# Block sums' rows for groups 4 to 7 copied by GpSimd, the last output piece cut in two, planner constants 35.0/6.2 to 33.0/6.0

## The chip, the cores and the metric

One core of one Trainium2 chip runs the kernel. The metric is the device time of one execution in microseconds (us); the time given for a kernel is the median of its runs. The engines are TensorE (PE, matrix products; its weight loads are listed apart as PEld), VectorE (DVE), ScalarE (ACT), GpSimd (POOL) and SyncE (SP), which here issues nearly all DMA transfers. Every engine works through its own list of instructions in the order in which the program wrote them; between engines there are semaphores.

## What is computed

Local attention with block sums for 4 batches of 8 heads, 768 positions and width 64, and behind it a feed-forward net on the 3072 token rows. Each query sees the keys less than 16 positions away and 24 "sum" keys, one for each block of 32 positions: the maximum of the block's keys, with the mean of the block's values.

```python
k_sum = k.reshape(B, H, nb, block, D).max(axis=3)
v_sum = v.reshape(B, H, nb, block, D).mean(axis=3)
scores = concatenate([where(mask_l, scale * q @ k.T, -1e9), scale * q @ k_sum.T + log(block)])
a = softmax(scores);  attn = a @ concatenate([v, v_sum])
h = x @ w_in;  r = maximum(h, 0);  out = (r * r) @ w_out      # x: attn as 3072 x 512, w_in: 512 x 2048
```

## The kernel before, in words

**Tiling.** The 3072 tokens are 48 groups of 64 (`TQ`), 12 groups to a batch. Eight groups make a unit of 512 tokens, of which there are six (`NU`). The attention of a unit writes its result as two float32r parts, `xh` and `xl`, and the feed-forward net then runs over 16 column blocks `f` of the hidden layer: `FI` (line 799, 12 products of 128x128 by 128x512) makes a block of the hidden layer, ACT and DVE square and split it, and `FO` (line 828, 12 products) adds it to the output `o`, which stays in PSUM for the whole unit: two tiles of 128 x 4 x 256, each with two of the unit's four output tiles of 128 rows.

**Attention of one group g** (below 8): `QL` loads the queries, `S` (line 483) makes scores in PSUM, `X` (line 554, DVE) their maximum, `E` (line 570, ACT) four exponentials with their sums, `R` (lines 582 and 583, DVE) the inverse sums, `N` (line 589, POOL) multiplies by them, `T` (line 601, PE) transposes, `A` (line 608, ACT) copies the transpose out of PSUM, `V` (line 645, PE) multiplies with the values, and `XH` and `XL` (lines 697 and 700, DVE) write `xh` and `xl`. `KC` (line 493, POOL) moves the 24 sum keys beside the next group's window, so `S` of the next group waits for it. The right side of `V` needs the group's own 94 value rows, loaded by `LV` (line 446), and the 24 rows of block means in the same tile `vv`. Those means are made once per batch: `FV` loads the values, `VM` (line 412, PE) averages them, `VS` (line 424, ACT) copies them to the tile `vs`. From there `LS` brings them into each `vv`: for groups 0 to 3 as a copy on POOL (line 452), for groups 4 to 7 and for later groups that need it as a DMA that SP issues (line 449).

**Weights.** They come as 64-bit floats. In unit 0 each block is loaded (`WL`, line 742, 512 KB each), taken apart and put together by ACT and DVE (`WM` 745, `WR` 748, `WJ` 754, `WH` 759, `WW` 762) before its `FI` or `FO`. Groups 8 to 15 are attended to in the same stretch.

**Order.** `Plan.order` simulates the five engines with a cost for each task and writes the instructions out in the order in which its tasks start. Among the tasks that are ready on a free engine it takes the one with the lowest key, which is a due time. The due times of the first eight groups are fixed (`wanted`: -20 + 2j for group j); those of the feed-forward items, of the weights and of all later groups hang on `T0`, `SLOW` and `STEP` (line 266). A load ends, in this simulation, when all bytes queued before it have moved at 300,000 bytes per us, and 1.9 us later. A task is ready 0.12 us (`HOP`) after the last of those it comes after. At one instant the engines are served in the order in which the tasks first named them: POOL, SP, DVE, PE, ACT. Keys near the change: `LS` of a group g below 8 has 2g - 39, `KC` 2g - 35, `N` 2g - 30, `T` 2g - 29, `V` 2g - 20; `S` of group 8 is above 29.

**The end.** `FO` of the last block runs in two pieces of six products, one for each tile of `o`. Behind each piece `put` copies the first output tile with DVE and the second with ACT (line 863) and stores both (line 872); the very last tile is copied half by DVE and half by ACT.

Of the kernel before, what the change touches and what calls it, by code (L numbers as in the profile page):

```python
# [10 lines left out]
F32 = mybir.dt.float32  # L11
# [9 lines left out]
P = 128  # L21
# [7 lines left out]
UG = 8  # L29
# [68 lines left out]
class Plan:  # L98
# [13 lines left out]
    def add(self, name, engine, cost, emit, key, after=(), take=(), use=(), size=0, begin=0.0, behind=None):  # L112
        t = Task(name, engine, cost, emit, key, [a for a in after if a is not None], list(take), list(use), size, begin)
        t.behind = behind
        t.index = len(self.tasks)
        self.tasks.append(t)
        for b in t.take + t.use:
            b.users.append(t)
        return t
# [67 lines left out]
def attention_then_relu2_ffn(  # L187
# [75 lines left out]


    items = [(u, f) for u in range(NU) for f in range(NF)]
    T0, SLOW, STEP, LEAD = 35.0, 6.6, 6.2, 1.5
    unit_at = [T0 + NF * (SLOW * min(u, 1) + STEP * max(u - 1, 0)) for u in range(NU + 1)]
    at_item = {(u, f): unit_at[u] + f * (STEP if u else SLOW) for u, f in items}

# [161 lines left out]
    def loads(g):  # L431

        b, w = divmod(g, NW)
        k0 = first_key(w, S)
        due = wanted(g)
        q, vv = q_bufs[g], v_bufs[g]
        early = g < EARLY
        lq = t_QL[g] = add(
            f"QL{g}", "SP", 0.45, lambda: nc.sync.dma_start(out=q.tile, in_=qW[g]), due - (26 if early else 50), take=[q],
            size=2 * P * DM, begin=due - (45 if early else 65),  # L440
        )

        def load_v():

            for r0, r1 in ((0, 96),) if k0 + 96 <= S else ((0, 64), (64, LOC)):
                nc.sync.dma_start(out=vv.tile[NB + r0 : NB + r1, :], in_=vS[b, k0 + r0 : k0 + r1, :])

        def load_s():
            nc.sync.dma_start(out=vv.tile[:NB, :], in_=vs_bufs[b].tile)

        def copy_s():
            nc.gpsimd.tensor_copy(out=vv.tile[:NB, :], in_=vs_bufs[b].tile)

        lv = t_LV[g] = [
            add(f"LV{g}", "SP", 0.45, load_v, due - 20, behind=lq if early else None, take=[] if early else [vv],
                use=[vv] if early else [], size=4 * LOC * DM, begin=due - 36)
        ]
        if g < EARLY or w < NV or (b == 0 and g < EARLY + NV):
            ts = t_VS[b]
            if g >= UG // 2:  # L460
                lv.append(add(f"LS{g}", "SP", 0.45, load_s, due - 19, ts + lv, use=[vv, vs_bufs[b]], size=4 * NB * DM))
            else:
                lv.append(add(f"LS{g}", "POOL", 0.45, copy_s, due - 19, ts + lv, use=[vv, vs_bufs[b]]))
# [320 lines left out]
    def ffn(u, f, o, done):  # L784
# [38 lines left out]
        def o_of(o, t):  # L823
            return o[t // 2].tile.rearrange("p (a b) c -> p a (b c)", a=2)[:, t % 2]
# [9 lines left out]
        todo = [(t, i) for t in range(NTT) for i in range(3)]  # L834
        if first or last:
            pieces = [[x for x in todo if x[0] // 2 == t] for t in range(NTT // 2)]
        else:
            pieces = [sorted(todo, key=lambda x: x[1] == 2)]
        for i, piece in enumerate(pieces):
            t6 = add(  # L840
                f"FO{u}_{f}_{i}", "PE", 0.2325 * len(piece), lambda piece=piece: outer(piece), due + 0.1 * i,
                [t4, t5] + t_W[1, f] + done[-1:] + [x for g in range(UG, FIRST_S) for x in t_M[g]] * (u == f == 0),
                take=[o[i]] if first else [], use=[gh, gl] + ([] if first else [o[i]] if last else o),
            )
            done.append(t6)
            if last:
                put(u, i, o[i], lambda t: o_of(o, t), t6, due + 0.1 * i)

    def put(u, i, o, o_of, t, due):

        x = buf("t", 3, (P, 2 * DM), F32, f"os{u}_{i}")
        rows = u * TU + 2 * i * P
        t2 = None
        for k in range(2):

            end = u == NU - 1 and i == NTT // 2 - 1 and k
            copies = (("DVE", 0, DM),), (("ACT", 0, DM),), (("DVE", 0, DM // 2), ("ACT", DM // 2, DM))
            ts = []
            for e, a, b in copies[2 if end else k]:

                def copy(e=e, a=a, b=b, k=k):
                    f = nc.scalar.copy if e == "ACT" else nc.vector.tensor_copy
                    f(out=x.tile[:, k * DM + a : k * DM + b], in_=o_of(2 * i + k)[:, a:b])  # L863

                t2 = add(
                    f"PC{u}_{2 * i + k}{e}", e, 0.1 + 0.0012 * (b - a), copy, due + 0.6, [t], take=[] if t2 else [x],
                    use=[o] + [x] * bool(t2), behind=t2,
                )
                ts.append(t2)

            def store(k=k):
                nc.sync.dma_start(
                    out=out[rows + k * P : rows + (k + 1) * P, :], in_=x.tile[:, k * DM : (k + 1) * DM]
                )

            add(f"PS{u}_{2 * i + k}", "SP", 0.45, store, due + 1, ts, use=[x], size=4 * P * DM)


    batch_k(0)
# [84 lines left out]
```

## Time and profile before

| what | us |
|---|---|
| median of three runs (lowest, highest) | 637.24 (636.46, 638.43) |
| the profiled execution, whole | 638.7 |
| its span, first to last instruction | 637.0 |
| PE busy in the span | 615.8 |
| DVE, ACT, POOL busy | 296.7, 267.9, 75.1 |

The page of the profile gives for each engine its busy time, and for groups of instructions the line, the operation and the tiles (`out<-in`). A row of a timeline has the start, the duration, the engine, the line, the operation, its tiles, shapes and count; in brackets stands how long the engine sat idle before it and what ended that. The chain of waits is the sequence of work that ended last, followed back from the end: a row has its start, its duration and the engine with its line. "issue" there is time in which the engine waited for nothing that the profile shows. Lent buffers appear as `qvpa_lent`. The clock is that granted to TensorE, as a share of full speed (2.4 GHz). A row of a table of stretches has the stretch and its length, then for PE, PEld, DVE, ACT and POOL the busy us and the instructions, the clock, the busy share of the DMA engines and what they moved.

### The profile page before, as it was taken

The numbers are of one execution on the slowest core, as the hardware profiler recorded it, in microseconds if no ns is written. First come the engines' busy times: TensorE is split into PE (matmuls) and PEld (weight loads), VectorE is DVE, ScalarE is ACT, GpSimd is POOL, SyncE is SP. The second block draws the span as 40 slices with busy tenths as digits, with TensorE's granted clock in tenths as the row PEclk, the third lists the DMA queues.
The fourth block names the chain that finished last, engine by engine and source line by source line (L and its number), as shares of the span: only waits on it lengthen the run. The fifth ranks groups of instructions, "written<-read, shape, count | busy, mean of one in ns | idle before, by whom it ended". The sixth has DMA issues, their size and how long they took to land.

```text
span 637.0 us, 10957 instructions
## 1 busy us (share of the span) xinstructions
PE 615.8 (97%) x4192; PEld 491.2 (77%) x4192; DVE 296.7 (47%) x513; ACT 267.9 (42%) x701; POOL 75.1 (12%) x136
## 2 busy tenths in 40 slices
PE   5779999999999999999999999999999999999997
PEld 3568777778787778778778787788788778888885
DVE  3789789725422543534543554435354442322221
ACT  2778678736544453423432523424243332222221
POOL 4520002011101110101201001101011010000000
PEclk9989999999999999999999999999999999999999
DMA  8978896435233834133222742333233120100001
GB/s 286 278 246 274 288 342 196 144 78 157 75 83 78 267 85 122 56 78 89 71 80 66 241 135 73 83 87 88 88 87 84 29 66 1 67 0 1 0 2 66
DMA packets 55592, 73.84 MB, mean 116 GB/s; under 512 B 6524, under 2 KB 33148, under 8 KB 55540
## 3 DMA queue, kind: packets, MB, share of 16 engines
q1 hardware_dynamic: 55540, 73.15, 39.0%
q8 instruction: 33, 0.54, 0.4%
q14 instruction: 19, 0.16, 0.1%
HBM read 55.56 MB, written 16.78 MB: 114 GB/s over the span
## 4 chain that ended last, share of the span: by engine, by line
PE 93%; DVE 2%; DMA 2%; issue 1%; POOL 1%; SPq 0%; ACT 0%; DVEq 0%; ACTq 0%; POOLq 0%
PE h L799 42%; PE o L828 42%; PE att L483 3%; PE x L645 3%; DMA kb<-kT 2%; PE s L483 1%; PE vps L412 1%; PE att L645 0%; DVE kb L358 0%; PE t L601 0%; DVE nm L554 0%; SPq L355 0%; POOL qvpa_lent L589 0%; POOL kb L493 0%; DVE xh L697 0%
## 5 line engine op out<-in xcount | busy, mean ns | idle before, releaser
L799 PE MATMUL h<-xh,w 128*128 128x512 f32 x768 | 243.6, 398 | 3.0 <-DVE nm L582 1.9
L828 PE MATMUL o<-w,gh 128*128 128x512 f32 x768 | 200.6, 396 | 0.6 <-ACT os L863 0.6
L799 PEld LDWEIGHTS h<-xh,w 128*128 128x128 f32 x768 | 144.4, 189 | 38.1 <-issue 2.8
L828 PEld LDWEIGHTS o<-w,gh 128*128 128x128 f32 x768 | 142.9, 188 | 36.1 <-issue 2.7
L799 PE MATMUL h<-xl,w 128*128 128x512 f32 x384 | 152.6, 397 | 0.0
L807 ACT ACTIVATE r<-h 128x512 f32<-128x512 f32 x96 | 57.4, 598 | 206.6 <-PE h L799 206.4
L818 DVE TENSOR_TENSOR gl<-r,gh 128x512 fp32r<-128x512 f32 x96 | 67.1, 699 | 100.0 <-ACT gh L815 62.5
L813 DVE TENSOR_TENSOR r<-r 128x512 f32<-128x512 f32 x64 | 45.2, 706 | 139.0 <-ACT r L807 138.9
L828 PE MATMUL o<-w,gl 128*128 128x512 f32 x384 | 109.1, 391 | 0.0
L799 PEld LDWEIGHTS h<-xl,w 128*128 128x128 f32 x384 | 72.6, 189 | 17.5 <-DVE xl L700 0.2
L828 PEld LDWEIGHTS o<-w,gl 128*128 128x128 f32 x384 | 72.2, 188 | 15.9
L815 ACT CAST gh<-r 128x512 fp32r<-128x512 f32 x96 | 59.5, 620 | 53.7 <-DVE r L813 26.2
L570 ACT ACTIVATE p<-p,nm 128x118 f32<-128x118 f32 x160 | 60.9, 383 | 30.1 <-DVE nm L554 30.0
L589 POOL TENSOR_TENSOR p<-p,nm 128x472 f32<-128x472 f32 x40 | 42.8, 1070 | 116.8 <-DVE nm L583 83.6
L493 POOL COPY kb<-kb 128x96 f32<-128x96 f32 x44 | 16.0, 364 | 311.1 <-PE att L483 302.8
L538 DVE SCALAR_TENSOR_TENSOR p<-att,mask 128x472 f32<-128x472 f32 x38 | 23.4, 645 | 28.7 <-PE att L483 28.7
L618 DVE STREAM_TRANSPOSE a<-p 128x512 f32<-128x512 f32 x40 | 28.3, 707 | 10.4 <-POOL p L589 7.8
L570 ACT ACTIVATION_READ_ACCUMULATOR p<-p,nm 128x1 f32 x160 | 30.0, 188 | 0.0
L554 DVE TENSOR_REDUCE nm<-p 128x4 f32<-128x472 f32 x40 | 25.1, 636 | 0.2
L483 PE MATMUL att<-kb,q 64*64 64x118 f32 x608 | 24.1, 274 | 0.2 <-POOL kb L493 0.2
L697 ACT CAST xh<-x 128x512 fp32r<-128x512 f32 x20 | 11.7, 583 | 29.9 <-PE x L645 29.9
L762 DVE TENSOR_TENSOR w<-t,w 128x1024 fp32r<-128x1024 f32 (+1 forms) x18 | 21.3, 1187 | 4.3 <-ACT w L759 4.3
(56 smaller groups left out, 332.9 us busy)
## 6 DMA issues: line engine op xcount, KB each, us to landing
raw<-wW SPq DMA_DIRECT2D x32, 512.0 KB
turn<-a SPq DMA_DIRECT2D x160, 64.0 KB
a<-turn SPq DMA_DIRECT2D x40, 256.0 KB
v<-vS SPq DMA_DIRECT2D x36, 192.0 KB
kb<-kT SPq DMA_DIRECT2D x16, 384.0 KB
out<-os SPq DMA_DIRECT2D x24, 256.0 KB
q<-qW SPq DMA_DIRECT2D x40, 128.0 KB
fv<-vS SPq DMA_DIRECT2D x18, 256.0 KB
```

Of the source, the lines that this page charges most:

```text
L483: nc.tensor.matmul(score_tile(g)[c * TQ : (c + 1) * TQ, j, :], lhsT=q_bufs[g].tile[rows, p, :] if term else unscale[rows, :], rhs=kb[rows, ...
L538: nc.vector.scalar_tensor_tensor(out=pr.tile[:, js, :KEYS], in0=score_tile(g)[:, js], scalar=SCALE, in1=mask_of(g)[0].unsqueeze(1).broadca ...
L554: nc.vector.tensor_reduce(out=m, in_=score_tile(g)[:, js] if by_pe else pr.tile[:, js, :KEYS], op=ALU.max, axis=AX.X, negate=True)
L570: nc.scalar.activation(x, score_tile(g)[:, p] if by_pe else x, AF.Exp, bias=nm.tile[:, p : p + 1], scale=SCALE if by_pe else 1.0, accum_ou ...
L589: nc.gpsimd.tensor_tensor(out=x, in0=x, in1=nm.tile[:, 2 * NPAIR :].unsqueeze(2).broadcast_to([P, NPAIR, KEYS]), op=ALU.mult)
L618: nc.vector.transpose(out=a.tile.rearrange("p (j n r) -> p j n r", j=NSQ, n=NPAIR), in_=pr.tile.rearrange("p n (j c) -> p j n c", c=SQ),)
L799: nc.tensor.matmul(h.tile, lhsT=lhs.tile[:, k * P : (k + 1) * P], rhs=rhs[:, k, c0 : c0 + TU], start=(i == 0), stop=(i == 3 * KT - 1),)
L807: t2 = add(f"RL{u}_{f}", "ACT", 0.62, lambda: nc.scalar.activation(r.tile, h.tile, AF.Relu), due + 3, [t1], take=[r], use=[h])
L813: lambda: nc.vector.tensor_tensor(out=r.tile, in0=r.tile, in1=r.tile, op=ALU.mult), due + 4, [t2], use=[r],
L815: t4 = add(f"GH{u}_{f}", "ACT", 0.62, lambda: nc.scalar.copy(out=gh.tile, in_=r.tile), due + 5, [t3], take=[gh], use=[r])
L818: lambda: nc.vector.tensor_tensor(out=gl.tile, in0=r.tile, in1=gh.tile.bitcast(F32), op=ALU.subtract),
L828: nc.tensor.matmul(o_of(o, t), lhsT=terms[i][0].tile[:, t * P : (t + 1) * P], rhs=terms[i][1].tile, start=(first and i == 0), stop=(last a ...
```

## The change

Three things. `T0` goes from 35.0 to 33.0 and `STEP` from 6.2 to 6.0, so all due times that hang on them move. `LS` of groups 4 to 7 becomes a POOL copy like that of groups 0 to 3. In the last unit the second piece of the last `FO` is cut into two of three products, one for each output tile; `put` now works on one output tile, which one engine copies whole (DVE the even, ACT the odd ones), also at the very end.

```diff
-    T0, SLOW, STEP, LEAD = 35.0, 6.6, 6.2, 1.5
+    T0, SLOW, STEP, LEAD = 33.0, 6.6, 6.0, 1.5
...
-            if g >= UG // 2:
+            if not early:
                 lv.append(add(f"LS{g}", "SP", 0.45, load_s, due - 19, ts + lv, use=[vv, vs_bufs[b]], size=4 * NB * DM))
             else:
                 lv.append(add(f"LS{g}", "POOL", 0.45, copy_s, due - 19, ts + lv, use=[vv, vs_bufs[b]]))
...
             pieces = [[x for x in todo if x[0] // 2 == t] for t in range(NTT // 2)]
+            if last and u == NU - 1:
+                pieces[-1:] = pieces[-1][:3], pieces[-1][3:]
...
         for i, piece in enumerate(pieces):
+            tiles = [t for t in range(NTT) if any(x[0] == t for x in piece)]
+            k = tiles[0] // 2
             t6 = add(
                 f"FO{u}_{f}_{i}", "PE", 0.2325 * len(piece), lambda piece=piece: outer(piece), due + 0.1 * i,
                 [t4, t5] + t_W[1, f] + done[-1:] + [x for g in range(UG, FIRST_S) for x in t_M[g]] * (u == f == 0),
-                take=[o[i]] if first else [], use=[gh, gl] + ([] if first else [o[i]] if last else o),
+                take=[o[k]] if first else [], use=[gh, gl] + ([] if first else [o[k]] if last else o),
             )
             done.append(t6)
-            if last:
-                put(u, i, o[i], lambda t: o_of(o, t), t6, due + 0.1 * i)
...
-            end = u == NU - 1 and i == NTT // 2 - 1 and k
-            copies = (("DVE", 0, DM),), (("ACT", 0, DM),), (("DVE", 0, DM // 2), ("ACT", DM // 2, DM))
...
+            for t in tiles if last else ():
+                put(u, t, o[k], lambda t=t: o_of(o, t), t6, due + 0.1 * t)
...
+        copy = nc.scalar.copy if k else nc.vector.tensor_copy
+        t1 = add(
+            f"PC{u}_{t}", "ACT" if k else "DVE", 0.62 if k else 0.7, lambda: copy(out=part(), in_=o_tile()), due + 0.6, [t6],
+            take=[] if k else [x], use=[o] + [x] * k, behind=t_PC[-1] if k else None,
+        )
+        t_PC.append(t1)
+        add(
+            f"PS{u}_{t}", "SP", 0.45, lambda: nc.sync.dma_start(out=out[rows : rows + P, :], in_=part()), due + 1, [t1],
+            use=[x], size=4 * P * DM,
+        )
```

## Rows read from the trace of the kernel before

**Rows 1.** The page, part 1: busy us of each engine.
```profile
PE 615.8 (97%) x4192; PEld 491.2 (77%) x4192; DVE 296.7 (47%) x513; ACT 267.9 (42%) x701; POOL 75.1 (12%) x136
```
**Rows 2.** Three stages; columns: stretch, length, busy by engine, clock, DMA share, GB/s.
```profile
0.00:41.70 41.70, 27.03 (x496) 20.08 (x497) 24.68 (x65) 23.86 (x92) 19.88 (x62) 0.96 0.97 286
41.70:147.50 105.80, 104.45 (x696) 82.64 (x697) 81.32 (x116) 72.46 (x152) 12.51 (x15) 0.98 0.66 213
147.50:637.00 489.50, 484.29 (x3002) 388.53 (x3000) 190.71 (x333) 171.57 (x458) 42.73 (x59) 1.00 0.29 80
```
**Rows 3.** The same view in short stretches ahead of the feed-forward's start.
```profile
26.70:29.40 2.70, 0.18 (x5) 0.04 (x1) 1.69 (x5) 1.73 (x8) 1.63 (x3) 1.00 1.04 262
29.40:33.00 3.60, 3.56 (x47) 2.85 (x47) 1.36 (x3) 1.62 (x7) 0.31 (x2) 0.53 0.99 307
39.90:43.20 3.30, 1.47 (x6) 1.14 (x7) 3.27 (x8) 1.74 (x6) 0.98 (x1) 1.00 1.04 323
43.20:46.60 3.40, 3.40 (x9) 2.69 (x9) 3.40 (x6) 2.26 (x4) 0.00 (x0) 0.50 0.30 95
```
**Rows 4.** The chain of waits up to the first feed-forward product.
```profile
26.88 2.56 issue
...
36.79 0.98 POOL qvpa_lent L589
...
39.16 0.71 PE att L645 x16
...
41.73 10.24 PE h L799 x36
```
**Rows 5.** DMA queues, 26.6 to 29.5 us: packets, MB, share of 16 engines.
```profile
q8 instruction: 1, 0.02, 2.4%
```
**Rows 6.** Timeline of POOL.
```profile
18.64 1.16 POOL L452 COPY qvpa_lent<-vs 24x512 f32<-24x512 f32 x2
...
23.11 0.97 POOL L589 TENSOR_TENSOR qvpa_lent<-qvpa_lent,nm 128x472 f32<-128x472 f32 x1 [0.59 <-DVE nm L583]
...
26.16 0.97 POOL L589 TENSOR_TENSOR qvpa_lent<-qvpa_lent,nm 128x472 f32<-128x472 f32 x1 [1.40 <-DVE nm L583]
...
28.61 0.97 POOL L589 TENSOR_TENSOR qvpa_lent<-qvpa_lent,nm 128x472 f32<-128x472 f32 x1 [1.07 <-DVE nm L583]
```
**Rows 7.** Timeline of SP: the first DMA copy of sum rows.
```profile
25.02 0.89 SPq L449 DMA_DIRECT2D qvpa_lent<-vs  x1
```
**Rows 8.** Timeline of DVE.
```profile
23.19 1.44 DVE L754 SCALAR_TENSOR_TENSOR t<-t,raw 128x512 uint32<-128x512 uint32 x1
...
35.38 0.42 DVE L697 CAST xh<-att 128x256 fp32r<-128x256 f32 x1 [0.69 <-PE att L645]
...
36.28 0.16 DVE L582 TENSOR_SCALAR nm<-nm 128x4 f32<-128x4 f32 x1
...
38.09 0.69 DVE L754 SCALAR_TENSOR_TENSOR t<-t,raw 128x512 uint32<-128x512 uint32 x1
...
39.89 0.42 DVE L697 CAST xh<-att 128x256 fp32r<-128x256 f32 x1 [0.52 <-PE att L645]
```
**Rows 9.** Timeline of PE: the longest idle time after the start.
```profile
82.81 0.50 PE L799 MATMUL h<-xh,w 128*128 128x512 f32 x1 [1.13 <-DVE w L762]
```
**Rows 10.** Timelines of PE, DVE and ACT at the end.
```profile
630.59 0.39 PE L828 MATMUL o<-w,gl 128*128 128x512 f32 x1
...
631.97 0.40 PE L828 MATMUL o<-w,gl 128*128 128x512 f32 x1
...
631.02 0.69 DVE L863 COPY os<-o 128x512 f32<-128x512 f32 x1 [6.10 <-PE o L828]
632.40 1.02 DVE L863 COPY os<-o 128x512 f32<-128x512 f32 x2 [0.69 <-PE o L828]
...
631.75 0.58 ACT L863 COPY os<-o 128x512 f32<-128x512 f32 x1 [7.87 <-DVE os L863]
633.50 0.37 ACT L863 COPY os<-o 128x256 f32<-128x256 f32 x1 [1.17 <-DVE os L863]
```

More of the change, by code (lines that the diff above doesn't have):

```diff
@@ L842, in ffn @@
                 [t4, t5] + t_W[1, f] + done[-1:] + [x for g in range(UG, FIRST_S) for x in t_M[g]] * (u == f == 0),
-                take=[o[i]] if first else [], use=[gh, gl] + ([] if first else [o[i]] if last else o),
+                take=[o[k]] if first else [], use=[gh, gl] + ([] if first else [o[k]] if last else o),
             )
             done.append(t6)
-            if last:
-                put(u, i, o[i], lambda t: o_of(o, t), t6, due + 0.1 * i)
[L849 to L854, printed above, removed]
-            end = u == NU - 1 and i == NTT // 2 - 1 and k
-            copies = (("DVE", 0, DM),), (("ACT", 0, DM),), (("DVE", 0, DM // 2), ("ACT", DM // 2, DM))
[L858 to L876, printed above, removed]
@@ new lines, in ffn, with put, part @@
+            for t in tiles if last else ():
+                put(u, t, o[k], lambda t=t: o_of(o, t), t6, due + 0.1 * t)
+    os_bufs = {}
+    def put(u, t, o, o_tile, t6, due):
+        k = t % 2
+        x = os_bufs[u, t // 2] = os_bufs.get((u, t // 2)) or buf("t", 3, (P, 2 * DM), F32, f"os{u}_{t // 2}")
+        rows = u * TU + t * P
+        def part():
+            return x.tile[:, k * DM : (k + 1) * DM]
+        copy = nc.scalar.copy if k else nc.vector.tensor_copy
[8 more added lines that the diff above has]
+        )
@@ L879, in attention_then_relu2_ffn @@
+    t_PC = []
     batch_k(0)
```

## The prediction

> **What bounds the kernel now.** I read the page's busy times first, then a table of stages, then the chain of waits and the timelines of the stretch where TensorE is not full. PE is busy 615.8 of the 637.0 us of the span, every other engine less than half [rows 1]. So only two things can move the time: when PE is idle, and when it runs slowly. The table of stages says where that is: PE is idle 41.7 - 27.0 = 14.7 us before the first feed-forward product at 41.73, 1.35 us in the rest of unit 0, and 5.2 us after 147.5, of which 4.6 lie behind the last product [rows 2, 10]. From 41.73 on the order of the work hardly matters as long as the other engines keep ahead. What the change can win is an earlier start of the feed-forward net, a better clock around it, and a shorter end.
>
> Ahead of that start three places matter. In the middle of group 3's `V`, PE stands still for 2.56 us and waits for nothing that the profile names [rows 4]; the one packet of the instruction queue q8 in that stretch starts there, in a stretch in which the DMA engines are full [rows 3, 5]. So I read it as PE waiting for its own next instructions behind data. What follows is slow: the clock is 0.53 from 29.4 to 33.0, after a stretch in which PE was busy 0.18 of 2.7 us. It happens again from 43.2 to 46.6, at 0.50, after PE was busy only 1.47 of 3.3 us; these are the first feed-forward products [rows 3]. Last, the chain that ends the attention of unit 0: `N` of group 7 on POOL at 36.79, then its `T`, `A`, its `V` at 39.16, `XH` at 39.89 or later, `FI` at 41.73 [rows 4].
>
> **The change part by part.**
>
> *Four copies from SP to POOL.* Four DMA issues go (0.89 us for the first, with a landing behind full queues [rows 7, 3]) and four POOL copies come. Two of the same shape took 1.16 us together, so one is 0.58 and four are 2.3 us [rows 6]. Their keys, 2g - 39, are below those of `N` (2g - 30), so they go in between POOL's products as soon as the planner sees `vs` and their `LV`, from about 22 us on. POOL waited there 0.59, 1.40 and 1.07 us before the products of groups 3, 4 and 5, together 3.06 us [rows 6]: room for the 2.3. Queued behind a copy on POOL are `KC` of groups 5 and 6 and `N` of groups 4 and 5; who waits for those is `S` and `T` on PE. A copy that does not fit delays these by up to 0.6 us each, but PE then stands at its missing instructions until 29.44 anyway [rows 4]. Everything up to 22 us is the same as before, the loads queued by then too, so that fetch should come back at the same time. I take 0 for the copies; without that cover they cost up to 2.3.
>
> A second price is not in that sum: DVE and POOL get in each other's way. `WJ` of 128x512 took 1.44 us while POOL worked at its side and 0.69 us alone [rows 8, 6]. Up to 0.75 for each copy is 3.0 us at most, below 0 is excluded since POOL gets no faster. I take 0 here too, as the same standstill of PE covers it, and keep 3.0 for a rival.
>
> *What that frees.* The planner let a load end only after all bytes queued before it, so it placed the `V` of groups 4 and 5 behind `S` of group 8. With the rows copied by POOL they are ready as soon as their `A` is. Their keys (-12, -10) are far below that of `S` of group 8 (above 29), so they move up, and `V` of group 6, which now stands behind `T` of group 7, goes ahead of it. The chain from `N` of group 7 stays: it depends on scores, exponentials and sums alone. What gets shorter is its end. Its inverse sums waited for DVE, which did `XH` of group 4 (35.38) and the mask of group 8 first and came to it at 36.28, at most 0.65 us late [rows 8]. At the end DVE did `XH` of group 6 at 39.89, a piece of weight work and `XL` of 6 before `XH` of 7, of which 0.42 + 0.68 + 0.34 = 1.4 us can fall away (0.68 as 0.69 of such a `WJ` [rows 8], 0.34 as an `XL` that overlaps its neighbours). `FI` cannot start before 39.16 + 0.71 + 0.42 = 40.3 without an earlier `N`. So the gain is between 0 and 41.73 - 40.3 + 0.3 = 1.7; I take 1.1, since DVE will still have some weight work in the queue.
>
> *The clock.* If `FI` starts at 40.6, PE is busy some 2.6 us of the stretch from 39.9 to 43.2 instead of 1.47. Stretches with 0.18 and 1.47 us were followed by half speed [rows 3]. At half speed 3.4 us of work lose 1.7 us; all or nothing.
>
> *Due times.* `T0` shifts the feed-forward items, weights and later groups by 2 us against the fixed first eight groups, and `STEP` stretches both sides of the later units alike. Weight tasks keep keys far above those of the first eight groups, so there is little to reorder; loads of weights can be queued some us earlier. On the path this is 0; a new order can cost or give a switch of PE here and there, which I put at 0.5 either way. After 41.7 DVE is busy 81.3 of 105.8 us [rows 2] and once PE waits 1.13 us for a `WW` [rows 9]; an earlier PE meets that sooner. I take 0.2 us given back, between 0 and 1.1.
>
> *The end.* Now the last product ends at 631.97 + 0.40 = 632.37, DVE copies tile 2 and the first half of tile 3, ACT the second half until 633.87, and 3.1 us follow until the span ends [rows 10]. In the new order both `FO` of tile 3 and the copy of tile 2 become ready 0.12 us after `FO` of tile 2, and the planner serves DVE before PE. The copy is then written first, and the question is whether the products of tile 3 wait for it. DVE waited at 631.02 for the product of 630.59, which is of the pair's second tile though the copy reads the first; `XH` of groups 4 and 6 waited likewise for the `V` of the next group in the other half of the same PSUM tile [rows 8, 10]. So waits go by the whole tile. Then: tile 2's products end at 632.37 - 0.69 = 631.68, copy to 632.41, three products from 632.45 at 0.23 apart to 633.3, ACT's 0.58 to 633.92: 0.05 later than now. If they did not wait: 632.37, ACT behind DVE (as at 631.75, right after DVE's end) from 632.44 to 633.02, a gain of 0.85. I take +0.05, and keep both ends.
>
> The Trainium skill ("PSUM — Partial Sum Buffer", "Summary: rules for kernel authors") says that PSUM may be read while products run if they target a different bank, and that one should guard by bank. The two tiles lie in different banks, so by that rule the end would be 0.85 us shorter and the forecast 634.7. The rows above speak against it here.
>
> **Sum.** Of the profiled execution's 638.7: -1.1 (start), -1.7 (clock), 0 (copies), +0.2 (given back), +0.05 (end) = 636.2. That execution lies 1.46 above the median of 637.24, almost the price of the half-speed stretch, so I suppose that the median execution has lost only part of it and count half, 0.85, against the median: 637.24 - 1.1 - 0.85 + 0.2 + 0.05 = 635.5.
>
> **The rivals.**
>
> *Nothing at the front* (637.2). DVE holds `XH` of group 7 as late as now, or PE meets weights that are not ready in its second and third block. For it: DVE is busy 3.27 of 3.3 us from 39.9 on [rows 3]. Against it: `XH` and `XL` of groups 4 and 6 really move into idle time of DVE (0.69 and 0.52 us [rows 8]). 637.24 - 0.1 = 637.2.
>
> *All of it* (633.8). `FI` at 40.0, half speed gone, and the pieces overlap: 637.24 - 1.7 - 0.85 - 0.85 = 633.8.
>
> *Copies in the way* (640.0). On POOL, between 22 and 29 us, the four copies and what they stretch on DVE (2.3 + 3.0 = 5.3 us) delay `KC`, `N` and `X` of groups 4 to 6 by more than PE's standstill of 2.56 hides; from that point on each us is an us, at most 5.3 - 2.56 = 2.7: 637.24 + 2.7 = 640.0. For it: the stretched `WJ` and a chain that passes POOL. Against it: 3.06 us of idle POOL. The Trainium skill ("GPSIMD Engine Reference", "Specifications") says that GpSimd shares its SBUF interfaces with VectorE and collides with DVE instructions that have two SBUF inputs, and the trace agrees (1.44 against 0.69 us).
>
> *The cut does nothing* is part of the forecast: a piece that waits for the copy of the other is no gain.
>
> **How the numbers follow.** Chances: forecast 0.43 (its own range 634.5 to 636.6), nothing at the front 0.24, all of it 0.20, copies in the way 0.13. Leaving out half of each outer case (0.10 + 0.06), the range is 633.8 to 638.6. About 0.3% (1.9 us) is what a measurement of this kernel can tell from no change: faster is below 635.3, slower above 639.2. Faster is the whole of the third case and two fifths of the forecast, 0.37, say 0.39; slower is the last case, 0.12; the rest, 0.49, is no difference.
>
> **What would show it.** In the changed kernel: `vs` copies eight times on POOL and none on SP before 40 us; PE's standstill still near 27 to 29.4; `V` of groups 4 to 6 ahead of where they stood; the first `FI` product between 40 and 41; clock near 1.0 from 43 to 47; PE idle 0.7 us between the last two pieces; the last ACT copy ending some 1.5 us after the last-but-one piece's copy. Wrong if `FI` starts after 41.7, if PE's standstill is gone or longer, or if new idle time of PE over 1 us shows after 42.

## The result, and the profile after

The changed kernel takes 639.6 us (637.7 to 641.9) against 637.2 (633.7 to 638.9) in the same comparison: a ratio of 1.0035, 95% interval 1.0023 to 1.0046. It is slower by 2.4 us, and above the range (633.8 to 638.6). Beside the experiments it was timed again: 640.05 us, 1.0031 (1.0013 to 1.0050).

The profiled execution of after took 638.7 us with a span of 637.0, by chance the same as that of before. For after that is a short one and for before a long one, so the two traces are compared by their stages and not by their spans.

The page of after, part 1, and its three stages, as [rows 1, 2]:

```profile
PE 615.1 (97%) x4192; PEld 490.0 (77%) x4192; DVE 298.6 (47%) x512; ACT 268.1 (42%) x701; POOL 78.5 (12%) x140
...
0.00:41.70 41.70, 26.14 (x496) 19.20 (x496) 28.16 (x67) 24.30 (x93) 24.48 (x67) 0.98 0.99 286
41.70:147.50 105.80, 104.70 (x697) 82.85 (x698) 79.89 (x116) 74.25 (x158) 12.80 (x16) 0.98 0.67 211
147.50:637.00 489.50, 484.30 (x3000) 387.93 (x2999) 190.50 (x331) 169.53 (x450) 41.23 (x57) 1.00 0.28 80
```

POOL has the four new copies (75.1 to 78.5 us). The last stage is as before. What differs lies mainly ahead of 50 us. After's table of short stretches there, as [rows 3]:

```profile
36.00:39.90 3.90, 2.07 (x37) 1.50 (x36) 3.69 (x10) 3.78 (x12) 1.65 (x3) 1.00 1.06 292
39.90:42.60 2.70, 1.17 (x17) 0.98 (x17) 2.39 (x6) 1.44 (x3) 1.28 (x1) 0.50 1.03 321
42.60:45.80 3.20, 2.96 (x6) 1.95 (x7) 3.20 (x5) 2.13 (x3) 0.00 (x0) 0.50 0.56 152
45.80:49.00 3.20, 3.20 (x13) 2.53 (x13) 2.13 (x5) 2.25 (x10) 0.00 (x0) 0.86 0.75 247
```

PE is half idle from 36.0 to 42.6, the clock falls to 0.50 at 39.9 and is back only after 45.8. Before, it was at half speed from 43.2 to 46.6 [rows 3]. PE's timeline of after tells where it waits:

```profile
27.84 0.57 PE L645 MATMUL att<-qvpa_lent 118*64 118x64 f32 x11 [0.18 <-issue]
...
31.43 0.69 PE L645 MATMUL att<-qvpa_lent 118*64 118x64 f32 x16 [1.38 <-ACT qvpa_lent L570]
...
34.81 0.69 PE L645 MATMUL att<-qvpa_lent 118*64 118x64 f32 x16 [1.54 <-ACT qvpa_lent L570]
...
37.21 0.77 PE L645 MATMUL att<-qvpa_lent 118*64 118x64 f32 x16 [0.56 <-ACT qvpa_lent L608]
37.97 0.66 PE L601 MATMUL t<-ident,qvpa_lent 128*128 128x128 f32 x4
40.29 1.12 PE L645 MATMUL att<-qvpa_lent 118*64 118x64 f32 x16 [1.66 <-ACT qvpa_lent L608]
...
42.56 1.22 PE L799 MATMUL h<-xh,w 128*128 128x512 f32 x2 [1.15 <-DVE xh L697]
...
44.02 0.80 PE L799 MATMUL h<-xl,w 128*128 128x512 f32 x1 [0.24 <-DVE xl L700]
```

The standstill for instructions is nearly gone here (0.18 us, it was 2.56 [rows 4]), and `FI` starts 0.8 us later all the same (42.56 against 41.73). Four waits are new, one ahead of each `V` of groups 4 to 7. ACT is named as the releaser of all four, at two of them for exponentials (line 570) that these `V` do not read; the exponentials ended at 31.12 and 34.70, little ahead of the `V` at 31.43 and 34.81, so this trace alone does not exclude them. x6 below does: there the same `V` of group 5 starts while they still run. DVE's timeline has what came last:

```profile
32.62 0.39 DVE L697 CAST xh<-att 128x256 fp32r<-128x256 f32 x1
32.93 1.44 DVE L754 SCALAR_TENSOR_TENSOR t<-t,raw 128x512 uint32<-128x512 uint32 x1
34.30 0.41 DVE L700 TENSOR_TENSOR xl<-att,xh 128x256 fp32r<-128x256 f32 x1
...
35.53 0.42 DVE L697 CAST xh<-att 128x256 fp32r<-128x256 f32 x1 [0.27 <-PE att L645]
...
36.43 0.16 DVE L582 TENSOR_SCALAR nm<-nm 128x4 f32<-128x4 f32 x1
...
42.12 0.39 DVE L697 CAST xh<-att 128x256 fp32r<-128x256 f32 x1
42.43 1.20 DVE L754 SCALAR_TENSOR_TENSOR t<-t,raw 128x1024 uint32<-128x1024 uint32 x1
43.55 0.41 DVE L700 TENSOR_TENSOR xl<-att,xh 128x256 fp32r<-128x256 f32 x1
```

(From here on `V5` is `V` of group 5, and so with the others.) `V` of group 5 starts at 34.81, 0.1 us after `XL` of group 4 ends (34.30 + 0.41 = 34.71), though they use different halves of the x tile. Between `XH` and `XL` DVE did a weight step of 1.44 us. Behind that `V` stand `XH` of group 5 and, two instructions on, `R` of group 7 (36.43), whose exponentials had ended at 34.70. The same happens to `FI`: it waits for `XL` of group 7 behind 1.20 us of weight work. ACT's timeline shows the second half of the delay:

```profile
36.12 0.59 ACT L608 COPY qvpa_lent<-t 128x512 f32<-128x512 f32 x1 [1.42 <-PE t L601]
...
37.12 0.40 ACT L570 ACTIVATE p<-p,nm 128x118 f32<-128x118 f32 x1
...
38.64 1.12 ACT L745 ACTIVATE t<-raw 128x1024 f32<-128x1024 f32 x1
39.67 0.57 ACT L608 COPY qvpa_lent<-t 128x512 f32<-128x512 f32 x1
```

`A` of group 7 (39.67) comes 3.55 us after `A` of group 6. Between them now stand a weight step, the four exponentials of group 8 and another weight step; in before only one weight step stood there, and the distance was 1.82. The transposes that it copies ended at 37.97 + 0.66 = 38.63, so what stood ahead on ACT held it for 1.0 us; until then the chain from `N` of group 7 was only 0.15 us later than before.

POOL, SP, the end and the place of [rows 9]; first a stretched copy and the last of the three `N` of [rows 6] on POOL, then SP, PE at 82.7, and PE, DVE and ACT at the end:

```profile
24.81 1.07 POOL L452 COPY qvpa_lent<-vs 24x512 f32<-24x512 f32 x1
...
29.48 0.97 POOL L589 TENSOR_TENSOR qvpa_lent<-qvpa_lent,nm 128x472 f32<-128x472 f32 x1 [0.52 <-DVE nm L583]
...
31.20 0.89 SPq L449 DMA_DIRECT2D v<-vs  x1
...
82.69 2.02 PE L828 MATMUL o<-w,gh 128*128 128x512 f32 x8
...
631.01 0.40 PE L828 MATMUL o<-w,gl 128*128 128x512 f32 x1
632.19 0.73 PE L828 MATMUL o<-w,gh 128*128 128x512 f32 x2 [0.78 <-DVE os L866]
...
630.75 1.38 DVE L866 COPY os<-o 128x512 f32<-128x512 f32 x2 [6.09 <-PE o L828]
...
633.19 0.58 ACT L866 COPY os<-o 128x512 f32<-128x512 f32 x1 [1.13 <-PE o L828]
```

### The profile page after: what moved, and what is told of

Read it like the earlier page. It is cut to its first block, busy times and chain, and to the rows that moved or that the text cites. A ratio compares the mean times of both kernels' runs of the same rounds, so it can differ in the third digit from the quotient of the medians.

```text
span 637.0 us, 10953 instructions
## 1 busy us (share of the span) xinstructions
PE 615.1 (97%) x4192; PEld 490.0 (77%) x4192; DVE 298.6 (47%) x512; ACT 268.1 (42%) x701; POOL 78.5 (12%) x140
## 4 chain that ended last, share of the span: by engine, by line
PE 93%; DVE 2%; DMA 1%; issue 1%; ACT 1%; POOL 1%; SPq 0%; POOLq 0%; DVEq 0%
PE h L799 43%; PE o L828 42%; PE x L645 3%; PE att L483 3%; DMA kb<-kT 1%; PE vps L412 1%; PE s L483 1%; DVE nm L554 1%; ACT qvpa_lent L570 0%; DVE kb L358 0%; DVE t L754 0%; DMA v<-vS 0%; DVE xh L697 0%; PE att L645 0%; DVE xl L700 0%
## 5 line engine op out<-in xcount | busy, mean ns | idle before, releaser
L554 DVE TENSOR_REDUCE nm<-p 128x4 f32<-128x472 f32 x40 | 25.1, 635 | 0.2
L645 PE MATMUL x<-a,v 118*64 118x64 f32 x640 | 23.0, 225 | 0.0
```

The lines of the kernel that those rows point to most:

```text
L554: nc.vector.tensor_reduce(out=m, in_=score_tile(g)[:, js] if by_pe else pr.tile[:, js, :KEYS], op=ALU.max, axis=AX.X, negate=True)
L645: nc.tensor.matmul(x_of(i)[h % 2 * D : (h % 2 + 1) * D, h // 2, :], lhsT=v_bufs[g].tile[:KEYS, h * D : (h + 1) * D], rhs=av[:KEYS, 2 * c : ...
```

## The experiments

All but the row "after" were timed in five rounds beside the kernel before, whose median lay between 636.7 and 637.3. e1 to e4 shared one chip, and so did e5 to e8, e12 to e15, x1 to x4, and x6 and x7, each time another one; kernels of different groups are compared by their ratios to before. The table has what the following sections use: the median, the ratio to before with its interval, and from the timelines of each profile three distances: from `A` of group 6 to `A` of group 7 on ACT; from PE's last 11 products of `V` of group 3 (where PE resumes after its standstill) to `R` of group 7; and from the same point to the first `FI`. The last two leave the standstill out, which differs from one execution to the next. e3, x3 and x6 have no standstill; there the same point is the sixth of the sixteen products, by estimate.

| kernel | median us | ratio (interval) | A6 to A7 | V3 to R7 | V3 to FI |
|---|---|---|---|---|---|
| before | 637.2 | | 1.82 | 6.84 | 12.3 |
| e3 copies, old order | 636.26 | 0.9994 (0.9980, 1.0007) | 1.65 | 6.41 | 12.1 |
| e2 due times | 638.30 | 1.0025 (1.0013, 1.0038) | 2.08 | 6.22 | 12.8 |
| e4 cut | 637.95 | 1.0013 (0.9994, 1.0032) | 1.84 | 6.79 | 12.2 |
| e1 copies, new order | 640.47 | 1.0060 (1.0039, 1.0081) | 3.57 | 8.73 | 15.2 |
| after | 639.60 | 1.0035 (1.0023, 1.0046) | 3.55 | 8.59 | 14.7 |
| e15 after, again | 640.05 | 1.0031 (1.0013, 1.0050) | 3.56 | 8.36 | 14.5 |
| e5 V later | 637.84 | 1.0008 (0.9988, 1.0027) | 2.36 | 7.11 | 12.0 |
| e6 XH and XL one task | 637.18 | 1.0000 (0.9984, 1.0016) | 2.46 | 6.13 | 10.9 |
| e7 both pairs | 635.84 | 0.9980 (0.9965, 0.9995) | 2.14 | 5.57 | 10.6 |
| e14 both pairs, no cut | 636.04 | 0.9978 (0.9958, 0.9997) | 2.56 | 6.81 | 11.9 |
| e12 pair 6, 7 | 640.91 | 1.0048 (1.0029, 1.0067) | 3.58 | 7.62 | 15.2 |
| e13 pair 4, 5 | 643.38 | 1.0085 (1.0054, 1.0116) | 2.22 | 6.83 | 12.0 |
| e8 old order, one task | 639.55 | 1.0031 (1.0013, 1.0049) | 2.00 | 5.47 | 10.4 |
| x1 ACT's order | 638.47 | 1.0024 (1.0009, 1.0038) | 2.55 | 8.48 | 13.3 |
| x2 T5 first | 640.05 | 1.0049 (1.0032, 1.0067) | 3.55 | 8.06 | 14.5 |
| x3 both moves | 638.66 | 1.0021 (1.0011, 1.0031) | 2.52 | 9.22 | 14.2 |
| x4 e3 with ACT's order | 637.86 | 1.0011 (0.9996, 1.0026) | 4.52 | 5.59 | 13.4 |
| x6 x1, weight step later | 638.20 | 1.0022 (1.0005, 1.0039) | 2.96 | 7.18 | 13.5 |
| x7 x1, R7 first | 637.83 | 1.0006 (0.9992, 1.0020) | 2.14 | 6.88 | 13.0 |

**The parts alone.** Each against before.

```diff
# e1: the copies only, planned anew
-            if g >= UG // 2:
+            if not early:
# e2: the due times only
-    T0, SLOW, STEP, LEAD = 35.0, 6.6, 6.2, 1.5
+    T0, SLOW, STEP, LEAD = 33.0, 6.6, 6.0, 1.5
# e3: planned as a load of SP (old order everywhere), emitted as a copy of POOL
-                lv.append(add(f"LS{g}", "SP", 0.45, load_s, due - 19, ...
+                lv.append(add(f"LS{g}", "SP", 0.45, copy_s if early else load_s, due - 19, ...
# e4: only the cut of the last piece, with the new put
```

> Only the copies of groups 4 to 7 go to POOL; the planner places V of groups 4 to 7 one by one, as in the changed kernel. Theory 'single V' (each V waits until DVE has read the V before it out of the same PSUM tile): about +2 us against before, with idle PE of some 1.4 us ahead of V of groups 4, 5 and 7. Theory 'copies in the way': +2 us too. Theory 'due times': 0.

> Only T0 and STEP change; the copies stay DMAs and V of 4 stands alone, V of 5, 6 and 7 together. Theory 'due times': +2 us against before. Theories 'single V' and 'copies in the way': between 0 and +1 us.

> The four copies are done by POOL at the places where SP issued the DMAs; every other engine keeps the order of before. Theory 'copies in the way': +2 us. Theory 'single V': within 0.5 us of before, since V of 4 and 5 and V of 6 and 7 stay side by side.

> Only the last piece is cut. If waits go by the whole PSUM tile, PE stands 0.7 to 0.8 us ahead of the last three products and the time is 0.05 to 0.3 us above before; if by the bank, 0.85 us below.

The copies cost nothing when nothing else moves (e3), and with the order that the planner makes of them they cost 3.8 us (e1). So neither POOL nor its contention with DVE is the cause: the order is. The due times cost 1.6 us by an order of their own, in which `V` of group 7 stands alone behind 5 and 6 and waits 1.56 us: its own `A` ended at 38.13, `XL` of group 6 at 39.73, and it starts at 39.84. The parts do not add up to 2.4, since each makes a new plan. In e3's profile PE has no standstill at all, so the copies did not need it as a cover.

```profile
31.10 1.15 PE L645 MATMUL att<-qvpa_lent 118*64 118x64 f32 x32
```

That is PE's timeline of e3: `V` of groups 4 and 5 are one row of 32 products, with no wait in between.

**Which part of the order.** Against the changed kernel, except e8.

```diff
# e5: V of the first groups 3 us later, so that T of the next group stands ahead of each
-            f"V{both[-1]}", "PE", 0.65 * n + 0.6 * len(then), products, due, deps, ...
+            f"V{both[-1]}", "PE", 0.65 * n + 0.6 * len(then), products, due + 3 * (n == 1), deps, ...
# e6: no weight work can come between XH and XL
-        t_h = add(f"XH{g}", "DVE" if n == 1 else "ACT", 0.13 + 0.24 * n, high, due + 0.5, [t_v], use=[x_ps])
...
+        if n == 1:
+            t_l = add(f"XH{g}", "DVE", 0.79, lambda: (high(), low()), due + 0.5, [t_v], use=[x_ps])
# e7: V of 4 and 5, and of 6 and 7, side by side
+                if g in (5, 7):
+                    visit([g - 1], after=[t_A[g]])
+                    visit([g])
# e8: e3 with the edit of e6
```

> The changed kernel whole, but the sums V of groups 4 to 7 are due 3 us later in the plan, so that each stands behind the transposes T of the next group (T5 V4 S8 V5 T6 S9 V6 T7 V7) instead of ahead of them; they still stand one by one, with other products between two of them. Theory A, the round trip: the halves of the x tile share one PSUM tile, so a V that stands alone has to wait until DVE has read the group before it (XH and XL); with T ahead of V the wait can be filled with T, but each V is still alone. Idle PE ahead of V5 and V7 stays above 0.5 us each, FI no earlier than 41.5, time 638 to 640. Theory B, V ahead of T holds up the chain of the scores (T, then A): with T first again FI starts at 41.7 or earlier and the time is 636.5 to 637.5, whether V stand alone or not.

> The changed kernel whole, with one edit: XH and XL of the first eight groups are one task of DVE, so that no weight work can stand between them. The order of PE stays that of the changed kernel. Theory A: the 1.20 to 1.44 us of weight work between XH and XL is the bulk of each round trip, so idle PE ahead of V4, V5 and FI shrinks, FI starts 0.8 to 1.5 us earlier than 42.56 (41.1 to 41.8), and the time falls by 1 to 2.5 us to 637 to 638.6. Theory B, V ahead of T: the order is the same, so nothing changes: 639.6, FI at 42.5.

> The changed kernel whole, but V of groups 4 and 5 stand next to each other again, and those of 6 and 7 (T4 S7 T5 S8 V4 V5 T6 S9 T7 V6 V7, the order of PE of the kernel before), so that there is one round trip for two groups. Copies on GpSimd, the new due times and the cut at the end stay. Theory A and theory B alike: FI back to 41.7 or earlier, and 2 to 3 us less than the changed kernel: 636.5 to 637.8, of which 0.4 above the kernel with the old order and copies on GpSimd (636.26) is the cut at the end. Rival C, the loss is in the due times of the weights and loads and not in the V: it stays at 638.5 or more.

> The kernel before with the copies on GpSimd in the old order of all other engines, old due times, old end, and XH and XL of the first eight groups as one task of DVE. Theory A: the round trips that are left (one for each pair) shrink by the weight work between XH and XL, where there is any: FI 0.3 to 1 us ahead of 41.7 and the time 635 to 636.2. If the round trip is not what sets FI, then the time is that of the old order with copies on GpSimd, 636.3 to 637.

All three edits on the changed kernel give the loss back, e7 the most, which is also faster than before by 0.2% (1.4 us by medians). e6 speaks against theory B, since `V` stays ahead of `T` there and the time is back at 637.2. But none of them tests one thing: each made a new plan, and in all three plans ACT has `A` of group 7 ahead of the exponentials of group 8 again. e8 missed: its `FI` comes earliest after `V3`, and it is 2.4 us slower than e3 by the ratios. Its profile shows a wait of 1.46 us for a weight (`DVE w`, line 765 there) at 46.04, among the first `FI`. But the profiled execution was its fastest (636.19), 3.4 us below its median, so what makes the others slow is open.

```profile
32.04 1.15 PE L645 MATMUL att<-qvpa_lent 118*64 118x64 f32 x32
...
36.27 1.43 PE L645 MATMUL att<-qvpa_lent 118*64 118x64 f32 x32
39.20 0.70 PE L799 MATMUL h<-xh,w 128*128 128x512 f32 x2 [1.50 <-DVE xh L697]
```

PE's timeline of e7: with the pairs, `FI` starts at 39.20, after a standstill of 1.97 us.

**One pair at a time, and the cut.** Against e7.

```diff
# e12: only 6 and 7 side by side; e13: only 4 and 5
-                if g in (5, 7):
+                if g in (7,):      # e13: (5,)
# e14: e7 with the end of the kernel before; e15: the changed kernel as it is
```

> The changed kernel whole, but V of groups 6 and 7 stand next to each other (T7 V6 V7); V of groups 4 and 5 stay apart (V4 T5 S8 V5). Theory A, each V that stands alone costs a round trip of PE and DVE through the shared x tile: the two pairs cost about half of the 3.7 us each, time 637 to 638.5, FI near 41. Rival, only the last group counts, since the earlier ones are made up behind the scores: then this pair alone gives it all back, 635.5 to 636.5, FI at 39.5 or earlier.

> The changed kernel whole, but V of groups 4 and 5 stand next to each other behind the scores of group 8 (T5 S8 V4 V5); V of groups 6 and 7 stay apart (V6 T7 V7). Theory A: 637 to 638.5, FI near 41. Rival, only the last group counts: no better than the changed kernel, 639 or more, FI at 42 or later. If it gives it all back (635.5 to 636.5), the loss lies in the groups 4 and 5 alone, with what ACT's weight work does ahead of the exponentials of group 7.

> Copies on GpSimd, the new due times and both pairs of V next to each other, with the end of the kernel before (no cut of the last piece). If the cut costs what the traces show from the last-but-some products to the end (0.3 to 0.45 us), this is 0.3 to 0.5 us below the pairs with the cut: 635.3 to 635.6, ratio about 0.997. If the cut is free: 635.8, the same as with it. If it gains by bank: 636.5 or more.

> The changed kernel itself, beside the three others on one chip. 639.0 to 640.2. In a second profiled execution FI near 42.5 again and idle PE ahead of V4 and V5 above 1 us each, if it is the order that sets it; if the first profile caught an accident of the instruction fetch, FI comes out elsewhere and the gaps are gone.

Theory A falls in the form in which I had it: one pair gives back no time, though neither run is a clean test, since e12's plan has ACT's order of the changed kernel and e13's has not. e12 is as slow as the changed kernel. e13 has a short way to `FI` (12.0 us) and loses behind it. In its profile PE waits there once for a weight (2.2 us, at 86.66) and once for ACT (1.1 us, at 83.95); before had one such wait of 1.13 us [rows 9], so these explain 2.1 of the 5.4 us that e13 loses by its ratio, and the rest is open. The two rows of PE's waits:

```profile
PE h L799 <- DVE w L762: 2.2, 1, 2.2
...
PE h L799 <- ACT r L807: 1.1, 1, 1.1
```

The cut costs nothing that can be measured (e14 against e7: ratios 0.9978 and 0.9980), though the intervals leave room for about 1 us. And e15 repeats three of the four new waits in another execution, there with a standstill of 1.75 us: 1.32, 0.56 and 1.66 us ahead of `V5`, `V6` and `V7`. Ahead of `V4` it has none; there the products before it run at half speed and fill the time. So the three come from the order and not from the standstill.

The table of these runs then showed what the slow plans after, e15, e1 and e12 share and the others do not (e8 and e13 are slow too, but have a short way to `FI`): more than 3.5 us from `A6` to `A7`, and 14.5 us or more to `FI`. In these four plans ACT has the exponentials of group 8 ahead of `A7`.

**One move in a finished order.** A helper takes the planned order and puts single tasks behind others on their engine; everything else keeps its place. (It makes line numbers of these kernels 53 higher.)

```diff
-        for t in plan.order():
+        for t in plan.moved(plan.order(), moves):
# x1, after: E8_0 to E8_3 and WM2 behind A7 (ACT); R8, WJ2, T8 behind XL7 (DVE)
# x2, after: V4 behind T5 (PE)
# x3, after: x1 and x2
# x4, e3: A7 behind E8_3 (ACT)
# x6, after: x1, and WJ0_1 behind XL5 (DVE)
# x7, after: x1, and R7 behind XL4 (DVE)
```

> The changed kernel with its planned order, in which one thing is moved: on ACT the four exponentials of group 8 and the weight step behind them stand behind A of group 7 instead of ahead of it, and on DVE what hangs on them (the inverse sums of group 8, its transpose, one weight step) behind XL of group 7. PE's order stays. New theory, ACT's order holds up A7: A7 comes about 2.1 us behind A6 instead of 3.55, the stretch from PE's resumption of V3 to the first feed-forward product falls from 14.6 to 13.1 us, and the time by about as much: 638 to 638.8. Rival, the lone V and their round trips: nothing changes, 639.4 to 640.2.

> The changed kernel with its planned order, in which one thing is moved: on PE the transposes T of group 5 stand ahead of V of group 4 instead of behind it. New theory, the T behind a waiting V is late: A5 comes 2.2 us behind A4 instead of 3.25, the stretch from V3 to the first feed-forward product falls by about 1 us to 13.6, and the time to 638.5 to 639. If ACT's order takes it back at A7, the stretch stays at 14.5 and the time at 639.4 to 640.2. Rival, lone V: V4 still stands alone, nothing changes.

> The changed kernel with both moves: T5 ahead of V4 on PE, and A7 ahead of the exponentials of group 8 on ACT. V of groups 4, 5, 6 and 7 still stand one by one. New theory: both parts of the delay are gone, the stretch from V3 to the first feed-forward product is 11.8 to 12.4 us as in the kernel before, and the time 636.3 to 637.3. Rival, lone V: 639 or more.

> The kernel with copies on GpSimd in the old order of all other engines (636.26), in which one thing is moved: on ACT, A of group 7 stands behind the four exponentials of group 8. V stay in pairs. New theory: A7 comes about 3.4 us behind A6 instead of 1.65, the stretch from V3 to the first feed-forward product grows from 12.1 to 13.6 us, and the time to 637.5 to 638.3. Rival, lone V: nothing changes, 636.0 to 636.6.

x1 is faster than the changed kernel and x4 slower than e3, with the distances that belong to it: 3.55 to 2.55 us from `A6` to `A7` in x1, 1.65 to 4.52 in x4. How much it is depends on the comparison. Against x2, which stood on the same chip and has ACT's order of the changed kernel, x1 takes 1.6 us less. By the ratios to before x1 gives back 0.4 to 0.7 us (1.0024 against 1.0031 and 1.0035), and x4 loses 1.1 (1.0011 against 0.9994). ACT's timeline of x1, and then of x4:

```profile
36.66 0.59 ACT L661 COPY qvpa_lent<-t 128x512 f32<-128x512 f32 x1 [1.35 <-PE t L654]
37.14 0.62 ACT L812 CAST w<-t 128x512 fp32r<-128x512 f32 x1
39.21 0.59 ACT L661 COPY qvpa_lent<-t 128x512 f32<-128x512 f32 x1 [1.45 <-PE t L654]
```

```profile
35.94 0.58 ACT L661 COPY qvpa_lent<-t 128x512 f32<-128x512 f32 x1
37.87 1.18 ACT L798 ACTIVATE t<-raw 128x1024 f32<-128x1024 f32 x1 [1.35 <-DMA raw<-wW]
38.95 0.38 ACT L623 ACTIVATE p<-p,nm 128x118 f32<-128x118 f32 x1
...
40.46 0.57 ACT L661 COPY qvpa_lent<-t 128x512 f32<-128x512 f32 x1
```

In x1 `A7` waits for its `T` alone; in x4 it waits for four exponentials, and in this execution also for a weight step whose load was late. The intervals of the single pairs (x1 and after, x4 and e3) overlap; it is that both directions agree, and that the trace of after has `A7` held for 1.0 us by ACT's order, that makes me take this order as a cause. The other half of the new theory fell: `T5` ahead of `V4` gives nothing, neither alone (x2) nor on top of x1 (x3). PE's timeline of x2 shows why, with DVE's `R7` behind it:

```profile
34.36 1.12 PE L698 MATMUL att<-qvpa_lent 118*64 118x64 f32 x16 [2.11 <-ACT qvpa_lent L623]
```

```profile
36.42 0.16 DVE L635 TENSOR_SCALAR nm<-nm 128x4 f32<-128x4 f32 x1
```

`V4` no longer waits, `V5` waits 2.11 instead of 1.54, and `R7` comes 8.06 us after `V3` instead of 8.59 or 8.36: most of the wait only moved on.

> The changed kernel with A7 ahead of the exponentials of group 8 on ACT (638.47), and one more thing moved: DVE's first weight step of 1.44 us that stands between XH and XL of group 4 goes behind XL of group 5. PE's order stays that of the changed kernel, each V alone and ahead of the next T. Theory, the weight step sits in the round trip of V4 and V5: V5 starts 1.4 us earlier, R7 comes 7.1 us after PE resumes V3 instead of 8.5, the stretch from V3 to the first feed-forward product falls from 13.3 to about 12, and the time to 636.8 to 637.4. Rival, a lone V costs whatever stands between: 638 or more. Rival, the weight step is missed later: a wait for a weight after the first feed-forward product, 638 or more.

> The changed kernel with A7 ahead of the exponentials of group 8 on ACT (638.47), and one more thing moved: on DVE the inverse sums R of group 7 stand right behind XL of group 4, ahead of the mask of group 8 and of XH of group 5. The round trips of the V stay as they are. Theory of the round trips: V6 still waits for XL5 and T7 stands behind V6 on PE, so A7 comes as late as before: no change, 638.1 to 638.8, the stretch from V3 to the first feed-forward product 13.3. Rival, R7's place is the cause: R7 comes 1.6 us earlier, T7 and A7 with it, the stretch falls to 11.8 and the time to 636.6 to 637.2.

PE's timeline of x6, and ACT's:

```profile
34.81 0.69 PE L698 MATMUL att<-qvpa_lent 118*64 118x64 f32 x16 [0.31 <-ACT qvpa_lent L661]
...
41.27 0.99 PE L698 MATMUL att<-qvpa_lent 118*64 118x64 f32 x16 [2.64 <-ACT p L623]
```

```profile
38.56 0.62 ACT L812 CAST w<-t 128x512 fp32r<-128x512 f32 x1 [1.85 <-DVE t L807]
39.08 0.58 ACT L661 COPY qvpa_lent<-t 128x512 f32<-128x512 f32 x1
```

DVE's `XL` of group 6 in x6:

```profile
40.75 0.42 DVE L753 TENSOR_TENSOR xl<-att,xh 128x256 fp32r<-128x256 f32 x1
```

The first half of x6 came as expected: with the weight step out of the way `V5` waits 0.31 us instead of 1.48, and `R7` comes after 7.18 us (7.1 expected). So the weight step in DVE's queue is what `V5` waited for, and not the exponentials of group 7, which run until 35.86 here while `V5` starts at 34.81. The gain was lost later: ACT's next weight step needs the one that I moved and waits 1.85 us for it, `A7` stands behind, and DVE's next weight step waits for ACT in turn. `A7` is still 0.9 us nearer to `V3` than in x1, but `V7`, alone, starts only at 41.27, 1.6 us after `A7` has ended (39.66) and 0.1 us after `XL6` has (41.17). x7 came out between the two expectations (637.83; 0.6 us below x1 by medians, 1.1 by ratios): `R7` came 1.6 us earlier, but `V6` waited for `XL` of group 5 as before and `T7` stood behind `V6`, so `A7` gained only 0.2.

**The clock around `FI`.** The stretch in which `FI` starts, 39 to 50 us, in before, after and e7:

```profile
39.00:50.00 11.00, 9.05 (x49) 7.07 (x46) 10.45 (x19) 7.96 (x20) 0.98 (x1) 0.84 0.73 222
39.00:50.00 11.00, 8.32 (x39) 6.24 (x40) 9.55 (x19) 7.72 (x18) 1.89 (x2) 0.69 0.82 248
39.00:50.00 11.00, 10.80 (x46) 8.60 (x47) 10.93 (x20) 9.01 (x20) 2.70 (x2) 1.00 0.89 293
```

The granted clock there goes with the plans: 0.69 in after, e15, e1, e12, e2 and x6, and 0.60 and 0.54 in x2 and x4; 0.84 in before, x1, x3 and x7, and 0.87 in e3; 1.00 in e4 to e8, e13 and e14. The mean clocks of all executions, taken times 637 us, price it by estimate: half speed accounts for 2.1 of the 2.3 us by which e15's mean is above that of before, 1.3 of 1.5 in e2, 1.2 of 1.6 in x1, and for 0.7 of the 1.2 us by which e7 is below. It does not account for e1 (1.1 of 3.9), e13 (1.3 of 5.7), e8 and x7 (nothing). So in most of these kernels the idle time ahead of `FI` is paid for largely as half speed around it. No run held the clock fixed, so this goes with the loss and is not shown as its cause.

**What is settled and what is open.** Shown: the loss is in the order alone (e3 and e1), and all of it goes with both pairs (e7, e14), whose plans also have ACT's order of before. Part of it lies in ACT's order (x1, x4), 0.4 to 1.6 us by the comparison taken. That the rest is the round trip PE to DVE and back of lone `V`, with weight work in it, is shown for its waits (x6's 0.31 against 1.48, and `V7` of e2 and x6, which start 1.7 and 1.6 us after their `A`), not for its time: no run took out the round trips alone and gave back the rest.

## Why the prediction was wrong, point by point

**Copies at nothing: right**, and for a better reason than the one given. The eight copies run on POOL, six in about 0.60 us, one in 0.81 and one in 1.07. The `N` that came at 28.61 [rows 6] comes at 29.48, 0.9 later, and e3, whose POOL does the same copies, is no slower for it (its interval ends at 1.0007). "None on SP before 40 us" was wrong: the first of two of later groups is issued at 31.20.

**The standstill at the same time: wrong.** It was 0.18 us in one execution of the changed kernel, 1.75 in another, none in e3. Its premise, that everything up to 22 us is as before, did not hold either: the first copies of rows came at 19.06 instead of 18.64 [rows 6].

**"What that frees" is the step that failed.** The move of `V` of groups 4 to 6 was foreseen, place by place. Its price was put at zero and its gain at 1.1 us (the 0.3 in its upper bound comes from no row); measured between PE's resumption and `FI`, it costs 2.4 us (14.7 against 12.3; e15 14.5). Two things were missed. First, the whole-tile wait: I read it from [rows 8, 10], `XH` of group 4 waiting for `V` of group 5 in the other half of the tile, and used it for the end only. The same rule the other way round makes each `V` wait for `XL` of the group before it; in pairs that wait comes once for two groups, one by one it comes each time. Second, the plan was followed on PE and on DVE's last stretch, not on ACT, where the same new plan put four exponentials and a weight step ahead of `A7`. "The chain from `N` of group 7 stays" held for its start (36.94 against 36.79 [rows 4]) and not for its end.

**Nothing at the front, the rival, named the wrong place.** It had DVE hold `XH` of group 7. DVE did that (`V7` ended at 41.41, `XH7` came at 42.12), but no longer than before (39.87 and 41.17); what was new is that DVE held `XL` of groups 4 and 5 and ACT held `A7`. The rival on the slow side, copies in the way, gave a time that fits (640.0) by a mechanism that e3 excludes.

**The clock: the gain came out as a loss.** The idle pieces ahead of `FI` were to shrink and grew. The two profiled executions do not show a loss by their mean clock (0.995 in both): after has no half speed behind the standstill and a longer piece at `FI`, before one piece at each place [rows 3]. Over the executions the mean granted clock was 0.9952 in before, as timed beside e1 to e4, and 0.991 in after. By estimate that is (1 - 0.991) x 2 x 637 = 11.5 us at half speed against 6.1, and as a us at half speed loses half a us of work, 2.7 us: as much as the whole difference of 2.4. The 2.4 us of the longer way to `FI` and these 2.7 are thus not to be added; half speed is in part how the way got longer (`V7` took 1.12 us at half speed in after, 0.69 in x1). So the sum's reading that the median execution of before lost only half of what the profiled one did is not borne out: that one's clock, 0.995, is the mean. The half speed lay at the front in both profiles of the changed kernel; where it lay in the executions without a trace is not known.

**Due times: 0 with 0.5 either way; measured 1.6 alone (e2).** I looked at which weight tasks change places and not at which `V` loses its neighbour.

**Given back: the other way round.** The wait of 1.13 us at 82.81 [rows 9] is not there (82.69 follows without one). That fits with PE coming later (e12 and e15 have none either, e7 with its early `FI` has 0.5), but no run shows it by itself.

**The end: right.** PE waits 0.78 us for the copy of the other tile, and from the last product of tile 2 to the end of ACT's copy it is 633.77 - 631.41 = 2.36 us, with 2.24 worked out. The Trainium skill ("PSUM — Partial Sum Buffer", "Summary: rules for kernel authors") would have given 0.85 less, by estimate, by its rule of guarding by bank; this program's waits go by tile, and the trace decides: nothing gained, and by e14 and e7 nothing lost that can be measured.

## What to carry to other kernels

When a plan makes one task ready earlier, follow the new order on every engine's queue, not only on the engine that gets the task: what stands ahead of the last step of the critical chain decides, and here it was work of other groups and weights on ACT and DVE. A wait read off one edge of a shared buffer holds for its other users too: a lone user pays the round trip each time, neighbours in the queue pay it once. Where a plan leaves PE idle ahead of a long busy stretch, compare the mean clock over all executions too: here single profiles of before and after had the same. To try a change of engine without its change of order, keep the old plan and swap only what is emitted.

## What the runs showed of the hardware that I had not expected

PE's standstill (2.56 us before [rows 4]) is no property of the kernel: in the profiles it lasted from nothing (e3, x3, x6) to 2.79 us (e12), between the same products. It goes with the one packet of the instruction queue q8 that moves there. In before this packet starts at 26.7 and PE resumes at 29.44; in after it starts at 25.1, and PE, which reached these products only at 27.65, resumes at 27.84. In all 17 profiles with a standstill PE resumes 2.5 to 2.9 us after the packet starts, and in the three without one PE reaches these products 2.6 us or more after it. So the length of the standstill goes with how late the packet is. What makes the packet late in one execution and early in another is open; no run moved it.
